# A new attention plan in a fused transformer block: V held still in four column tiles, row sums on VectorE, reciprocals through DRAM, and FFN chunks of 128 and 256 tokens

## The chip, the cores and the metric

The kernel runs on one core of one Trainium2 chip. The metric is the device time of a whole execution in microseconds (us); each figure is the median over the runs of a kernel. TensorE is called PE here, ScalarE ACT, VectorE DVE, GpSimd POOL, and SP is the engine that issues the DMA transfers. The *granted clock* is the share of full speed at which the chip let PE run.

## The reference, cut to what matters

One block with 2048 tokens of width 1024, all in bf16: layernorm, attention with 32 query heads of width 32 that share one key head and one value head, a residual, layernorm again, and a gated feed-forward network (FFN) of width 3584.

```python
q = (x @ wq) split into 32 heads          # x is the layernorm of A_x
k = x @ wk ; v = x @ wv                   # one head of width 32 for all
p = softmax(q @ k.T * 32 ** -0.5)         # 32 heads x 2048 x 2048
h = A_x + (p @ v) @ wo
g = layernorm(h) @ w_gate ; u = layernorm(h) @ w_up
out = h + (sigmoid(g) * u) @ w_down
```

The softmax takes 134 million exponentials. They are 1024 ACT instructions of 128 partitions x 1024 elements in both kernels.

## The kernel before

The Python that builds the kernel is a list scheduler: `pl.op(engine, instruction, deps, ...)` adds an operation with an assumed duration, and the scheduler fixes the order of instructions on every engine at build time. On the chip each engine runs its list in that order and waits on semaphores.

A *score visit* is one block of score matmuls followed by two exps. The exps write *slots* (tiles `Pr` in SBUF); a slot is free again when P V has read it. Scores have six PSUM banks. All other matmuls share two (`F_ps`), in *groups*: one group owns a bank until its result has been copied out. Score visits may come between any two matmuls of a group; another group may not.

Before, a slot holds 1024 elements per partition, and there are 16. Eight make a group of 4 heads x 128 queries. The probabilities are the stationary operand of P V, and the 33rd column of the moving V is ones, so the row sums come with the product and lie on the same partition as the queries that they divide:

```python
def mk_PV(G):
    def atoms(b):
        for j in range(4):                 # heads
            for kt in range(NT):           # 16 tiles of 128 keys
                mm(F_ps[:, b, j*VS : j*VS+DH+1], Pr[:, slot, co:co+P], Vaug[:, kt, 0:DH+1],
                   kt == 0, kt == NT - 1)
    def after(b, last):
        rL = DVE.reciprocal(ov[:, :, DH:DH+1])          # 4 elements a partition
        Osb = DVE.tensor_tensor(ov[:, :, 0:DH], rL broadcast, op=mult)
    first = lambda: [all exps of G] + [all of V]
    # (cut) a gate: V is complete, and earlier transposes are done; no reciprocal holds P V back
# (cut) then 4 PE transposes a half tile, a copy to OT, wo, layernorm,
# gate/up and down in 8 FFN chunks of 256 tokens
```

The loop that fills PE's list, the same in both kernels but for constants:

```python
while True:
    if can_s and run - t < 750.0: emit_S(v); v += 1; continue   # ACT nearly out of work
    if cur is not None: ...one more matmul of the running group...
    else: ...pick the first class in PRIO whose group is ready and whose gate is open...
    if can_s: emit_S(v) ...
# PRIO = xT, KV, Q0, PV, OTt, OP, hT, D, GU, Q;  can_s needs free slots
```

The softmax here doesn't subtract the row's maximum and nothing guards it: scores larger than these inputs give would overflow.

## Time and profile before

| | before |
|---|---|
| median of 2 runs | 1222.13 us (1219.03 to 1225.24) |
| span of the profiled run | 1223.8 us |
| PE / ACT / DVE busy | 96% / 85% / 26% |
| ACT's wait for scores | 25.9 us |
| start of the last exp | 1060.6 us |
| from the end of the last exp to the end | 162.2 us |

The page of the profiled run of the kernel before: its busy times, its busy tenths in 40 equal slices, and the exps' line (busy time, mean ns of one; then idle time before them and what ended it).

```profile
...
PE 1174.0 (96%) x22016; PEld 835.1 (68%) x22016; DVE 316.4 (26%) x838; ACT 1042.1 (85%) x1283; POOL 47.2 (4%) x109
...
PE   4899979999999999999999999999999999999999
...
DVE  8523321212222222223121222132222212232121
ACT  6899999999999999999999999999999989711120
...
PEclk9999989999999999999999999999999999999999
...
L495 ACT ACTIVATE Pr<-S_ps 128x1024 bf16<-128x1024 f32 x1024 | 972.4, 1052 | 26.4 <-PE S_ps L330 25.9
...
```

ACT is at eight or nine tenths until the 34th slice and, after the 35th, nearly idle, while PE goes on. The windows view of the same run, cut at the end of the last exp (busy us and instructions of each engine, then granted clock and DMA):

```profile
...
core 0: us, PE busy (x) PEld busy (x) DVE busy (x) ACT busy (x) POOL busy (x), PEclk, DMA share, GB/s
0.00:1061.60 1061.60, 1016.05 (x20773) 718.99 (x20774) 280.94 (x760) 1020.56 (x1227) 45.91 (x106) 0.99 0.41 117
1061.60:1223.80 162.20, 157.99 (x1245) 116.09 (x1243) 35.50 (x78) 21.54 (x57) 1.34 (x3) 1.00 0.63 164
...
```

ACT is busy for 1020.56 of the 1061.60 us of attention. The view of waits agrees (engine and line, then whom it waited for; us, times, longest):

```profile
...
engine line waited for: us in total, times, longest us
...
ACT Pr L495 <- PE S_ps L330: 25.9, 29, 2.2
...
```

PE's timeline after the last exp (start, duration, instructions):

```profile
...
1074.47 47.32 PE L330 MATMUL F_ps<-hnT,ring 128*128 128x256 bf16 x432
...
1123.48 24.34 PE L330 MATMUL F_ps<-zone,hact 128*128 128x512 bf16 x112
1147.65 49.07 PE L330 MATMUL F_ps<-hnT,ring 128*128 128x256 bf16 x448
1196.56 24.34 PE L330 MATMUL F_ps<-zone,hact 128*128 128x512 bf16 x112
```

These are gate/up and down of the last two chunks, dense. So attention is bounded by ACT, and the tail is PE work that did not fit beside it.

### The profile page before, as it was taken

What the parts mean: (1) busy time and instruction counts of PE and PEld (TensorE: products, weight loads), DVE (VectorE), ACT (ScalarE), POOL (GpSimd) and SP (SyncE); (2) the same over time, 40 slices, a digit from 0 to 9 for tenths busy, and PEclk for the clock granted to TensorE, in tenths of its full rate; (3) what the DMA queues carried; (4) which work ended last, traced back from release to release, by engine and by line L of the source; (5) the groups of instructions that cost most, each with busy time, mean ns of one, the idle gap of its engine ahead of it and who ended that gap; (6) DMA issues with size and microseconds to landing.
All of it is one profiled execution on the core that took longest, in us unless ns stands there. A gap on an engine that the chain in (4) does not pass through costs nothing.

```text
span 1223.8 us, 47137 instructions
## 1 busy us (share of the span) xinstructions
PE 1174.0 (96%) x22016; PEld 835.1 (68%) x22016; DVE 316.4 (26%) x838; ACT 1042.1 (85%) x1283; POOL 47.2 (4%) x109
## 2 busy tenths in 40 slices
PE   4899979999999999999999999999999999999999
PEld 3665557785678756877568675778657776587684
DVE  8523321212222222223121222132222212232121
ACT  6899999999999999999999999999999989711120
POOL 6100000000000000000000000000000000000000
PEclk9999989999999999999999999999999999999999
DMA  9411175562056601565016460256303653089390
GB/s 320 116 28 41 42 260 156 148 173 64 20 149 174 192 20 46 150 191 148 16 50 191 119 170 20 70 165 184 111 20 86 172 148 102 15 224 263 105 252 18
DMA packets 258612, 151.02 MB, mean 123 GB/s; under 512 B 7280, under 2 KB 248944, under 8 KB 258416
## 3 DMA queue, kind: packets, MB, share of 16 engines
q1 hardware_dynamic: 258416, 148.00, 43.1%
q8 instruction: 173, 2.83, 1.0%
q14 instruction: 23, 0.19, 0.0%
HBM read 140.64 MB, written 7.34 MB: 121 GB/s over the span
## 4 chain that ended last, share of the span: by engine, by line
PE 63%; ACT 31%; issue 3%; DVE 2%; POOL 0%; DMA 0%
PE F_ps L330 54%; ACT Pr L495 28%; PE S_ps L330 9%; ACT tnh L669 1%; ACT zone L313 1%; PE F_ps L619 0%; ACT zone L230 0%; DVE OT L566 0%; DVE st L274 0%; DVE st L276 0%; PE F_ps L558 0%; DMA ring<-in_A_x_dram 0%; POOL dsb L287 0%; DVE hnT L625 0%; DVE ring L307 0%
## 5 line engine op out<-in xcount | busy, mean ns | idle before, releaser
L495 ACT ACTIVATE Pr<-S_ps 128x1024 bf16<-128x1024 f32 x1024 | 972.4, 1052 | 26.4 <-PE S_ps L330 25.9
L330 PE MATMUL F_ps<-hnT,ring 128*128 128x256 bf16 x3584 | 440.6, 275 | 2.5 <-DVE OT L566 1.2
L330 PEld LDWEIGHTS F_ps<-hnT,ring 128*128 128x128 bf16 x3584 | 332.5, 98 | 61.3 <-issue 3.1
L330 PEld LDWEIGHTS F_ps<-Vaug,Pr 128*128 128x128 bf16 x8192 | 229.7, 96 | 28.1 <-issue 4.1
L330 PE MATMUL F_ps<-Vaug,Pr 128*128 128x33 bf16 x8192 | 244.4, 178 | 2.4 <-issue 1.5
L330 PE MATMUL S_ps<-QTb,kT 32*128 32x128 bf16 x8192 | 208.5, 218 | 15.4 <-ACT Pr L495 10.1
L330 PE MATMUL F_ps<-zone,hact 128*128 128x512 bf16 x896 | 213.2, 380 | 0.8 <-DVE OT L566 0.5
L330 PEld LDWEIGHTS S_ps<-QTb,kT 32*128 32x128 bf16 x8192 | 119.2, 93 | 127.9 <-ACT Pr L495 81.6
L676 DVE SCALAR_TENSOR_TENSOR hact<-tnh,F_ps 128x256 bf16<-128x256 f32 x224 | 94.3, 421 | 384.0 <-ACT tnh L669 383.9
L669 ACT ACTIVATE tnh<-F_ps 128x256 f32<-128x256 f32 x224 | 90.7, 405 | 115.0 <-PE F_ps L330 115.0
L330 PEld LDWEIGHTS F_ps<-zone,hact 128*128 128x128 bf16 x896 | 79.2, 98 | 91.3 <-DVE OT L566 0.7
L330 PE MATMUL F_ps<-zone 128*128 128x256 bf16 (+2 forms) x512 | 76.5, 292 | 3.1 <-POOL rstd L290 1.2
L707 DVE SCALAR_TENSOR_TENSOR h_sb<-F_ps,h_sb 128x512 bf16<-128x512 f32 x32 | 22.1, 692 | 203.1 <-PE F_ps L330 203.1
L330 PE MATMUL F_ps<-wo_sb,OT 128*128 128x512 bf16 x256 | 64.2, 381 | 3.8 <-DVE OT L566 3.7
L531 DVE RECIPROCAL rL<-F_ps 128x4 f32<-128x4 f32 x128 | 23.4, 183 | 133.7 <-PE F_ps L330 133.5
L330 PEld LDWEIGHTS F_ps<-zone 128*128 128x128 bf16 x512 | 37.5, 98 | 24.2 <-ACT zone L230 1.4
L284 POOL TENSOR_SCALAR zb<-mvb 128x1 bf16<-128x1 bf16 x32 | 7.5, 233 | 1026.4 <-DVE mvb L280 1026.1
L330 PEld LDWEIGHTS F_ps<-wo_sb,OT 128*128 128x128 bf16 x256 | 21.0, 97 | 28.4 <-DVE OT L566 6.9
L533 DVE TENSOR_TENSOR Osb<-F_ps,rL 128x128 bf16<-128x128 f32 x128 | 37.2, 291 | 3.8
L594 DVE TENSOR_TENSOR h_sb<-F_ps,xres 128x512 bf16<-128x512 f32 x32 | 22.1, 692 | 54.4 <-PE F_ps L330 54.4
L337 PE MATMUL F_ps<-ident,zone 128*128 128x128 bf16 x128 | 11.0, 236 | 17.3 <-POOL dsb L287 9.1
L231 DVE CAST hact<-F_ps 128x512 bf16<-128x512 f32 x24 | 16.6, 692 | 40.2 <-PE F_ps L330 40.2
(39 smaller groups left out, 232.4 us busy)
## 6 DMA issues: line engine op xcount, KB each, us to landing
ring<-in_B_w_gate_dram SPq DMA_DIRECT2D x112, 512.0 KB, 4.1
ring<-in_B_w_up_dram SPq DMA_DIRECT2D x112, 512.0 KB, 5.9
zone<-in_B_w_down_dram SPq DMA_DIRECT2D x4, 1792.0 KB, 15.4
ring<-in_A_x_dram SPq DMA_DIRECT2D x16, 256.0 KB, 7.0
xres<-in_A_x_dram SPq DMA_DIRECT2D x16, 256.0 KB, 2.7
out_dram<-h_sb SPq DMA_DIRECT2D x32, 128.0 KB, 1.7
q_scratch<-hact SPq DMA_DIRECT2D x24, 128.0 KB, 1.8
QTb<-q_scratch SPq DMA_DIRECT2D x6, 512.0 KB, 6.3
```

Of the source, the lines that this page charges most:

```text
L231: lambda: DVE.tensor_copy(out=out_ap, in_=in_ap))
L284: f = pl.op("pool", lambda: POOL.tensor_scalar(out=zb[:, ph, t:t + 1], in0=mvb[:, ph, t, 1:2], scalar1=LN_EPS_BF16, scalar2=None, op0=ALU. ...
L313: xnorm[t] = evac(lambda: ACT.activation(out=dst, in_=src, func=ACTF.Copy, scale=sc), lambda: DVE.tensor_scalar(out=dst, in0=src, scalar1= ...
L330: return lambda: PE.matmul(o, lhsT=l, rhs=r, start=start, stop=stop, **kw)
L337: return [(lambda dt=dt: PE.transpose(out=tp[:, dt * P:(dt + 1) * P], in_=xn[:, t % 2, dt * P:(dt + 1) * P], identity=ident[:, :]), P, []) ...
L495: exps[u] = pl.op("act", lambda slot=slot, pb=pb: ACT.activation(out=Pr[:, slot, :].rearrange("p (a b) -> p a b", a=2), in_=S_ps[:, pb:pb ...
L531: a = pl.op("dve", lambda: DVE.reciprocal(rL[:, k, :].unsqueeze(2), ov[:, :, DH:DH + 1]), [last], prio=0, occ=70, lat=280)
L533: e = pl.op("dve", lambda: DVE.tensor_tensor(out=Osb[:, hh % 2, (g % 4) * P:(g % 4 + 1) * P].rearrange("p (a b) -> p a b", a=4), in0=ov[:, ...
L594: h_ev[(t, dc)] = pl.op("dve", lambda: DVE.tensor_tensor(out=h_sb[:, t % 4, sl], in0=F_ps[:, b, :], in1=xres[:, t % 2, sl], op=ALU.add), [ ...
L669: a = pl.op("act", lambda: ACT.activation(out=tnh[:, k, :], in_=F_ps[:, b, 0:256], func=ACTF.Tanh, scale=0.5), [last, tn_user.get(k)], pri ...
L676: e = pl.op("dve", lambda: DVE.scalar_tensor_tensor(out=hactT[:, ft, :], in0=tnh[:, k, :], scalar=1.0, in1=F_ps[:, b, 256:512], op0=ALU.ad ...
L707: e = pl.op("dve", lambda: DVE.scalar_tensor_tensor(out=h_sb[:, t % 4, sl], in0=F_ps[:, b, :], scalar=0.5, in1=h_sb[:, t % 4, sl], op0=ALU ...
```

## The change

Its intent is to make P V cheaper on PE and to shorten the ends.

- V becomes the stationary operand, 32 columns wide, so four heads run side by side in four column tiles of the array and the moving operand is 256 probabilities. The product comes out transposed, as `wo` needs it, and the transposes of O go away.
- The ones column goes with it. DVE adds the probabilities of a group over the key tiles, a small group of matmuls (SUM) sums over partitions, and the reciprocals, which now lie on the wrong partitions, are broadcast through DRAM.
- A group is 8 slots of twice the size (4 heads x 256 score columns), and there are 12 slots (five more, in buffers that are not yet in use, serve at the start only). P V may be picked only when the reciprocals are nearly back by the builder's reckoning or, with at most one slot free, as soon as their load back has been issued there.
- The FFN's chunks are 128 tokens at both ends and 256 between, nine in place of eight.

The core of the diff, with cuts marked:

```diff
-    NPS = 16
+    NP = 12
-        Pr = SB("Pr", [NPS, 1024])
+        Pr = SB("Pr", [NP, 2048])
+        acc = SB("acc", [2, 2048])
 ...
+    add_op[(qi, kp, i)] = pl.op("dve", DVE.tensor_tensor(out=a, in0=in0, in1=slot[:, h], op=ALU.add), ...)
 ...
+    # SUM, then:
+    rc = pl.op("dve", DVE.reciprocal(r_sb[:, k, :], F_ps[:, b, 0:64]), ...)
+    r1 = dma(SP.dma_start(r_dram[k], r_sb[0:P:8, k, :]), ..., [rc], prio=0)
+    lds = [dma(SP.dma_start(rb[:, k, :], bass.AP(r_dram.tensor, r_dram.offset + k * 1024,
+               [[256, 4], [0, DH], [1, 256]])), ..., [r1, ot_ev.get(qi - 2)], prio=0)]
 ...
+    # P V, for kt, for j in 4 heads:
+    mm(F_ps[DH*j:DH*(j+1), b, 0:256], Vt[:, kt, :], s[:, j*512 + k2*256 : ...+256],
+       kt == 0, kt == NT - 1, tile_position=(0, DH * j))
+    def gate():
+        if qi not in rb_ld or any(o.end is None for o in rb_ld[qi]): return False
+        if len(free_slots) <= 1: return True
+        return rb_ld[qi][-1].end <= pl.free["pe"] + 1900.0
 ...
+    FC = [(0,)] + [(i, i + 1) for i in range(1, NT - 1, 2)] + [(NT - 1,)]
-    PRIO = ["xT", "KV", "Q0", "PV", "OTt", "OP", "hT", "D", "GU", "Q"]
+    PRIO = ["xT", "KV", "Q0", "SUM", "PV", "OP", "hT", "D", "GU", "Q1", "Q"]
-                if can_s and run - t < 750.0:
+                if can_s and run - t < 1000.0:
```

Left out here: the wider tanh (512 elements), layernorm statistics for several tiles at once, the order of the first loads, gate and up weights in quarters of a slab that are spaced out in time, three slabs for four, and the scheduler's assumed durations.

## The prediction

> **What bounds it now.** Two engines in turn. By the page, PE is busy 96% and ACT 85% of 1223.8 us. By the timelines the first score exp starts at 27.3 us and the last ends near 1061.6 us; in between ACT waits for scores only 25.9 us in all (view of waits). Eight exps take 7.57 us, so 1024 take 969 us. PE always has work too; what does not fit beside attention is left over: from 1061 to 1221 us it runs gate/up of two token chunks (47.3 and 49.1 us) and down projections (24.3 us each). So attention is ACT-bound, and the 162 us tail is PE backlog.
>
> **PE, costed by start-to-start rates of the timeline.** Score block of 16: 0.33 us. Old P V: 64 matmuls in 1.61 us, 25 ns each, 206 us in all. Gate/up: 448 in 49.07 us, 109 ns each.
>
> - Removed: old P V 206 us; the 128 transposes of O, 0.056 us each, 7 us.
> - Added: new P V, 16 rounds of four column tiles; I assume the four overlap fully, at 109 ns a round (estimate from the gate/up rate): 112 us, plus about 10 us of mode switches. Row-sum matmuls: 64 groups at about 0.35 us, plus the two raw groups: 26 us.
> - Unchanged: score, FFN and wo columns.
>
> Net PE saving 65 to 75 us.
>
> **ACT.** The exps stay 1024 of 1024 elements. Tanh becomes 98 of 512 and 28 of 256, about 60 us against 69. Attention still ends at about 1060.
>
> **DVE.** About 868 bf16 adds of 1024. The Trainium skill ("VectorE: DVE Perf Modes", the perf-mode tier table) gives bf16 tensor_tensor in SBUF two elements a cycle; here a bf16 PSUM copy of 1024 takes 691 ns, so I take 0.6 to 0.7 us each: 520 to 600 us. DVE goes from 316 us (26%) to about 800 us (70%), not binding.
>
> **DMA.** Nine FFN chunks instead of eight read 14.7 MB more. Each of 64 groups sends its reciprocal through DRAM and back, about 5 us, hidden while P V of that group is held back. The broadcast read has an outer size of 4; the skill ("DMA: Bandwidth & Descriptors", the rules table) says that confines it to four DMA engines; nothing here shows that yet.
>
> **Tail.** The last chunk has 128 tokens: its gate/up is 25 us of PE but 11 MB not yet loaded, at the 260 GB/s seen in the old tail 42 to 54 us. Last sums, round trip, P V, wo and layernorm: about 17 us; gate/up 46 to 50; down 12; output 3: about 80 us.
>
> **Sum.** 1060 + 80 + about 5 of backlog = 1145 us; 1105 to 1190 in 8 of 10.
>
> **What would show it.** Exps still 0.95 us each and ending at 1050 to 1070; new P V near 1.8 us a group; adds under 0.7 us; last gate/up phase waiting on DMA, PE visibly idle in it; mean PE share below 96%.
>
> **What would make it wrong.** The reciprocal's round trip late behind weight loads holds one of only two spare PSUM banks; PE is in order, so scores and exps starve. Column tiles overlapping less than fully (a round over 150 ns takes back 40 us). Adds at one element a cycle (1.1 us) would make DVE the bound.
>
> Faster by over 2%: 0.85; within 2%: 0.09; slower: 0.06.

## The result, and the profile after

The changed kernel takes 1297.41 us (median of 2 runs, 1297.25 to 1297.57). Its results are correct. Executions over 1.5% slower than the fastest of the same kernel are left out of the means. Ratios in this text are the mean time of one kernel's fast runs over that of the other's of the same rounds, so not quite the ratio of the medians. Here it is 1.0611, with a 95% interval of 1.0545 to 1.0678: slower by 6%. The prediction of 1145 us and its range of 1105 to 1190 us are both wrong, and so is the direction.

The page of the changed kernel, the same lines as before and the new ones:

```profile
...
PE 1145.6 (88%) x16632; PEld 694.3 (54%) x16704; DVE 840.1 (65%) x1450; ACT 1028.1 (79%) x1167; POOL 48.6 (4%) x89
...
PE   6879867879998999979997999889997999799967
...
DVE  8659855667767676676757776676757775764111
ACT  4759977879988997899979997899879997994010
...
PEclk9989978989999999989998999989998999899999
...
L567 ACT ACTIVATE Pr<-S_ps 128x1024 bf16<-128x1024 f32 x1014 | 965.3, 1037 | 119.8 <-PE S_ps L367 114.0
L544 DVE TENSOR_TENSOR acc<-acc,Pr 128x1024 bf16<-128x1024 bf16 x744 | 497.9, 688 | 126.8 <-ACT Pr L567 123.8
...
L367 PE MATMUL F_ps<-Pr,Vt 128*32 128x256 bf16 x4056 | 160.8, 299 | 0.5 <-DVE h_sb L859 0.5
...
```

Each exp is as long as it was (1037 against 1052 ns; ten more stand under the names of other buffers), and the adds take 688 ns as assumed. What differs is that ACT's row is full of eights and sevens, and that the granted clock dips again and again. The windows view of the changed kernel, cut at its own last exp:

```profile
...
core 0: us, PE busy (x) PEld busy (x) DVE busy (x) ACT busy (x) POOL busy (x), PEclk, DMA share, GB/s
0.00:1179.20 1179.20, 1048.75 (x15725) 627.99 (x15792) 820.15 (x1412) 1019.16 (x1147) 47.22 (x86) 0.95 0.45 131
1179.20:1295.50 116.30, 96.88 (x909) 66.34 (x912) 19.99 (x39) 8.97 (x21) 1.34 (x3) 0.96 0.59 171
...
```

ACT does the same work during attention, 1019.16 us against 1020.56, but attention takes 1179.2 us in place of 1061.6. The difference of 117.6 us is idle ACT (160.0 against 41.0 us, with 1.4 us less work). The tail is 45.9 us shorter. 117.6 less 45.9 is 71.7 us, the difference of the two spans. The view of waits says what ACT waited for:

```profile
...
engine line waited for: us in total, times, longest us
ACT Pr L567 <- PE S_ps L367: 114.0, 76, 14.0
...
```

114.0 against 25.9 us is 88 of the 118. The rest is mostly at the start and in waits for FFN results.

Now to a place where it happens. The timeline of the changed kernel, all engines, from a group's last exp on (the first of the four exps in the top line); S_ps is a score visit, `acc,sel` the SUM group, `zone,hact` a down projection, `Pr,Vt` P V:

```profile
...
644.96 3.99 ACT L567 ACTIVATE Pr<-S_ps 128x1024 bf16<-128x1024 f32 x4
...
648.67 0.42 PE L367 MATMUL F_ps<-acc,sel 128*32 128x64 bf16 x32
...
649.02 0.40 PE L367 MATMUL S_ps<-QTb,kT 32*128 32x256 bf16 x8
649.17 0.56 DVE L608 RECIPROCAL r_sb<-F_ps 128x64 f32<-128x64 f32 x1 [1.86 <-PE F_ps L367]
649.32 4.70 ACT L567 ACTIVATE Pr<-S_ps 128x1024 bf16<-128x1024 f32 x5
...
650.79 0.52 SPq L610 DMA_DIRECT2D r_scratch<-r_sb  x1
...
651.48 0.40 PE L367 MATMUL S_ps<-QTb,kT 32*128 32x256 bf16 x8
...
652.87 5.99 PE L367 MATMUL F_ps<-zone,hact 128*128 128x512 bf16 x27 [0.50 <-DVE hact L807]
...
654.46 0.54 SPq L611 DMA_DIRECT2D rb<-r_scratch  x1
...
658.79 0.40 PE L367 MATMUL F_ps<-Pr,Vt 128*32 128x256 bf16 x8
...
659.13 0.40 PE L367 MATMUL S_ps<-QTb,kT 32*128 32x256 bf16 x8
...
659.58 2.86 ACT L567 ACTIVATE Pr<-S_ps 128x1024 bf16<-128x1024 f32 x3 [5.56 <-PE S_ps L367]
...
```

The group's last exp ends at 646.0 us, its row sums are done at 649.1 and their reciprocals at 649.7. The store to DRAM is issued at 650.8, the load back at 654.5. Where the builder picked PE's next group, P V's gate was still shut, so it picked a down projection of 28 matmuls, which starts at 652.87 us (one record is missing in the trace). Up to 658.79 us there is no score visit among them, although a visit may come between any two of its matmuls and ACT runs dry at 654.0 us. P V starts at 658.79, a visit follows after its first two rounds, and ACT has stood idle for 5.56 us. That is exactly what one expects if no slot was free until P V had released one.

It can be counted. A visit loads 8 blocks of score weights and a P V group 64 blocks of V, and the trace has the record of every load. At the start of 60 of the 64 P V groups exactly 12 visits had begun whose slots no P V had read: all slots were taken. ACT's idle time before the first exp after each of these 60 starts adds up to 78 us of the 114.0. From a group's last exp to the start of its P V it takes 8.2 us in the median, while the four spare slots keep ACT busy for 7.6 us (eight exps). Before the change it took 1.6 us in the median, and the spare slots were worth the same eight exps.

The builder itself says so. By the builder's own assumed durations the kernel before ends at 1207 us and the changed one at 1273 us, 62 of the 64 P V groups are picked with no slot free, and ACT is out of work with no slot free for 73 us. The builder knows neither the granted clock nor late transfers. By its durations the order alone gives 66 of the 72 us between the two spans, and for every kernel of the table below its plan ends only 0.2 to 3.0% before the measured time. The experiments test the slots on the chip.

### The profile page after: what moved, and what is told of

Its sections match the earlier page's. It is cut to its first block, busy times and chain, and to the rows that moved or that the text cites. A ratio compares the mean times of both kernels' runs of the same rounds, so it can differ in the third digit from the quotient of the medians.

```text
span 1295.5 us, 38388 instructions
## 1 busy us (share of the span) xinstructions
PE 1145.6 (88%) x16632; PEld 694.3 (54%) x16704; DVE 840.1 (65%) x1450; ACT 1028.1 (79%) x1167; POOL 48.6 (4%) x89
## 4 chain that ended last, share of the span: by engine, by line
PE 68%; ACT 11%; DVE 8%; DMA 7%; issue 6%; SPq 1%; DVEq 0%
PE F_ps L367 58%; ACT Pr L567 10%; PE S_ps L367 10%; DMA ring<-in_B_w_up_dram 3%; DVE acc L544 2%; DVE hact L807 2%; DMA rb<-r_scratch 2%; DMA r_scratch<-r_sb 1%; SPq L758 1%; DMA ring<-in_B_w_gate_dram 1%; DVE st L312 1%; DVE h_sb L859 1%; DVE st L314 0%; DMA out_dram<-h_sb 0%; DVE zone L253 0%
## 5 line engine op out<-in xcount | busy, mean ns | idle before, releaser
L567 ACT ACTIVATE Pr<-S_ps 128x1024 bf16<-128x1024 f32 x1014 | 965.3, 1037 | 119.8 <-PE S_ps L367 114.0
L544 DVE TENSOR_TENSOR acc<-acc,Pr 128x1024 bf16<-128x1024 bf16 x744 | 497.9, 688 | 126.8 <-ACT Pr L567 123.8
L367 PE MATMUL F_ps<-hnT,ring 128*128 128x256 bf16 (+1 forms) x4032 | 452.7, 264 | 42.9 <-DMA ring<-in_B_w_up_dram 13.7
L367 PE MATMUL S_ps<-QTb,kT 32*128 32x256 bf16 x4096 | 210.7, 281 | 51.1 <-ACT Pr L567 50.1
L367 PE MATMUL F_ps<-Pr,Vt 128*32 128x256 bf16 x4056 | 160.8, 299 | 0.5 <-DVE h_sb L859 0.5
L367 PEld LDWEIGHTS F_ps<-Pr,Vt 128*32 128x32 bf16 x4056 | 101.1, 104 | 52.1 <-issue 42.0
L807 DVE SCALAR_TENSOR_TENSOR hact<-tnh,F_ps 128x512 bf16<-128x512 f32 x98 | 67.1, 684 | 58.8 <-PE F_ps L367 57.3
L544 DVE TENSOR_TENSOR acc<-Pr 128x1024 bf16<-128x1024 bf16 x122 | 78.3, 664 | 10.0 <-ACT Pr L567 8.8
L367 PE MATMUL F_ps<-zone 128*128 128x512 bf16 (+3 forms) x563 | 75.4, 282 | 3.9 <-ACT QTb L252 1.3
L832 ACT ACTIVATE tnh<-F_ps 128x256 f32<-128x256 f32 x28 | 10.9, 390 | 78.6 <-PE F_ps L367 78.6
L834 DVE SCALAR_TENSOR_TENSOR hact<-tnh,F_ps 128x256 bf16<-128x256 f32 x28 | 11.6, 416 | 49.6 <-ACT tnh L832 49.6
```

The costliest lines, as they stand in the source:

```text
L367: return lambda: PE.matmul(o, lhsT=l, rhs=r, start=start, stop=stop, **kw)
L544: add_op[(qi, kp, i)] = pl.op("dve", lambda: DVE.tensor_tensor(out=a, in0=in0, in1=slot[:, h], op=ALU.add), [exp_of[(qi, kp, i)]] + dp, pr ...
L567: exps[u] = pl.op("act", lambda i=i, pb=pb: ACT.activation(out=slot[:, i * 1024:(i + 1) * 1024].rearrange("p (a b) -> p a b", a=2), in_=S_ ...
L807: e = pl.op("dve", lambda: DVE.scalar_tensor_tensor(out=hact[:, sg * 512:(sg + 1) * 512], in0=tnh[:, k, :], scalar=1.0, in1=F_ps[:, b, :], ...
L832: a = pl.op("act", lambda: ACT.activation(out=tnh[:, k, 0:256], in_=F_ps[:, b, 0:256], func=ACTF.Tanh, scale=0.5), [last, tn_user.get(k)] ...
L834: e = pl.op("dve", lambda: DVE.scalar_tensor_tensor(out=hact[:, sg * 256:(sg + 1) * 256], in0=tnh[:, k, 0:256], scalar=1.0, in1=F_ps[:, b, ...
```

## The experiments

Four explanations were on the table. **A**: the slots. A group keeps its 8 of 12 slots until P V, P V waits for the trip through DRAM and then behind whatever FFN group is running, and meanwhile the builder has no slot for a score visit. **B**: the trip is later on the chip than the builder reckoned, and the in-order PE stands still at a held bank. **C**: DVE, 65% busy, delays what PE needs. **D**: the 128-token chunks wait for weights. The first four kernels ran on one chip, the next four on another, the last three on a third, each beside the kernel before.

| run | median us | ratio to before (95%) | ACT's wait for scores, us | last exp starts, us |
|---|---|---|---|---|
| before | 1222.13 | 1 | 25.9 | 1060.6 |
| changed | 1297.41 | 1.0611 (1.0545 to 1.0678) | 114.0 | 1178.2 |
| e1_no_wait | 1292.71 | 1.0546 (1.0497 to 1.0594) | 108.5 | 1171.6 |
| e2_no_trip | 1215.81 | 0.9931 (0.9893 to 0.9969) | 29.7 | 1081.4 |
| e3_short_adds | 1297.97 | 1.0597 (1.0548 to 1.0647) | 112.4 | 1173.0 |
| e4_ten_slots | 1456.81 | 1.1902 (1.1851 to 1.1952) | 176.1 | 1351.4 |
| e5_not_held | 1300.98 | 1.0651 (1.0611 to 1.0691) | 56.8 | 1105.8 |
| e6_break_in | 1252.74 | 1.0252 (1.0217 to 1.0288) | 61.2 | 1116.7 |
| e7_pairs | 1275.17 | 1.0436 (1.0400 to 1.0472) | 110.3 | 1166.4 |
| e8_ones | 1221.48 | 0.9995 (0.9959 to 1.0031) | 17.6 | 1073.1 |
| e9_ones_pairs | 1179.99 | 0.9643 (0.9615 to 0.9672) | 23.8 | 1073.0 |
| e10_break_pairs | 1234.98 | 1.0102 (1.0067 to 1.0137) | 74.3 | 1123.9 |
| e11_no_pacing | 1173.95 | 0.9586 (0.9553 to 0.9618) | 25.3 | 1075.4 |

### Is the chip late, or is the order itself at fault?

```diff
-   in1=rb[:, qi % 2, :]...
+   in1=rstd[:, 0, 0:1] broadcast          # a constant; results wrong on purpose
+   # after the order is fixed: this multiply no longer waits for the load of rb
```

> The changed kernel with the very same instruction order, but the multiply that finishes P V reads a constant and no longer waits for the reciprocals that come back from DRAM (results wrong on purpose; the transfers still run). Theory A (the order itself starves ScalarE: score visits are not in the instruction stream where they are needed, because all slots for probabilities are taken): 1280 to 1298 us, ratio to the changed kernel at least 0.985, ScalarE still idle for about 100 us before score exps. Rival B (the round trip is later on the chip than the plan reckoned, so the spare PSUM bank is held and the in-order PE stands still): 1150 to 1220 us.

1292.71 us; ACT still waits 108.5 us for scores. The order was the same and the trip's lateness could no longer stop PE, so B is not the cause: the intervals of this run and of the changed kernel overlap, so the 4.7 us between the medians are not clear of noise.

### Does the trip through DRAM make the bad order?

```diff
-   r1 = dma(... r_dram <- r_sb ...); lds = [dma(... rb <- r_dram ...)]
-   rb_ld[qi] = lds
+   rb_ld[qi] = [rc]                       # the reciprocals are used where they lie
-   in1=rb...
+   in1=r_sb broadcast                     # wrong partitions: results wrong on purpose
```

> The reciprocals are used in SBUF where they are computed, with no trip through DRAM (results wrong on purpose, since they stand on the wrong partitions); the plan orders the instructions anew, so P V is no longer held back for the trip. Theory A: slots come free sooner, the last exp ends at 1065 to 1090 us in place of 1179, the wait of ScalarE for scores falls from 114 us to under 45, and the whole takes 1190 to 1225 us. Rival C (VectorE's adds or the four-column P V itself slow attention): still over 1260 us.

1215.81 us, 82 less than the changed kernel. The wait for scores fell to 29.7 us and the last exp starts 97 us earlier:

```profile
...
ACT Pr L567 <- PE S_ps L367: 29.7, 26, 10.5
...
```

All 12 slots are taken at the start of 8 P V groups, no longer of 60. The adds and the four-column P V are all still there, so C falls for the greater part here.

### Are DVE's adds in the way?

```diff
-   DVE.tensor_tensor(out=a, in0=in0, in1=slot[:, h], op=ALU.add)
+   DVE.tensor_tensor(out=a[:, 0:128], in0=in0[:, 0:128], in1=slot[:, h][:, 0:128], op=ALU.add)
```

> The changed kernel with the very same order, but each row-sum add on VectorE covers 128 elements in place of 1024 (results wrong on purpose), so VectorE loses some 450 us of work. Theory A: within 1.5% of the changed kernel, 1278 to 1300 us. Rival C (VectorE at 65% with adds in front of evacuations is what holds PE up): 1150 to 1230 us.

1297.97 us, no change. The larger group of adds took 162.7 us in place of 497.9, and the time did not notice. DVE is not what holds the changed kernel in this order.

### Is it the number of slots?

```diff
-    NP = 12
+    NP = 10
```

> The changed kernel with 10 slots for probabilities in place of 12, nothing else, ordered anew. Theory A: a group fills 8 slots, so only 2 are left for the next group while the first waits for its reciprocals; ScalarE's idle time before score exps rises by 100 us or more and the time is 1390 to 1480 us. Rivals B and C: slots are not the limit, 1290 to 1320 us.

1456.81 us, 159 more, for two slots. The wait of ACT for scores rose by 62 us only, less than the 100 expected; the last exp is 173 us later, and ACT's waits for the 512-wide gate products, counted apart, rose from 30.0 to 105.1 us. The time is inside the range that A gave and far from the other's. More than 12 slots cannot be tried in this layout: with 13 the kernel does not build, for want of room in SBUF.

### What if P V is not held back?

```diff
-   if qi not in rb_ld or any(o.end is None for o in rb_ld[qi]): return False
-   if len(free_slots) <= 1: return True
-   return rb_ld[qi][-1].end <= pl.free["pe"] + 1900.0
+   return qi in rb_ld
```

> The trip through DRAM is kept, but the rule that holds P V back until its reciprocals are due is dropped: P V may start as soon as its sums are done, and its result then waits in its PSUM bank for the reciprocals. Theory A1 (the holding rule costs the time): 1200 to 1235 us, ScalarE's wait for scores under 60 us. Theory A2 (the trip costs it in any place: the wait moves from the slots to one of two spare PSUM banks): 1260 to 1300 us, hardly any change, with PE waiting more on the multiply after P V.

1300.98 us, no gain, as A2 said, but not quite in A2's way: attention did get shorter (the wait for scores is 56.8 us, the last exp 72 us earlier), and the tail got as much longer. The timeline of this run, one P V and what follows on PE, with DVE's multiply that empties P V's bank:

```profile
...
610.30 1.93 PE L367 MATMUL F_ps<-Pr,Vt 128*32 128x256 bf16 x64
...
612.17 0.28 PE L367 MATMUL F_ps<-hnT,ring 128*128 128x256 bf16 x1
...
616.30 1.58 PE L367 MATMUL F_ps<-hnT,ring 128*128 128x256 bf16 x13
...
618.70 0.42 DVE L640 TENSOR_TENSOR OT<-F_ps,rb 128x256 bf16<-128x256 f32 x1 [1.32 <-DMA rb<-r_scratch]
...
619.27 0.93 PE L367 MATMUL F_ps<-hnT,ring 128*128 128x256 bf16 x7 [0.63 <-DVE OT L640]
...
```

P V starts at 610.30 us and its bank is emptied at 619.12, because the multiply waits for the DMA. For 8.8 us the FFN has one bank in place of two. Over the whole run:

```profile
...
PE F_ps L367 <- DVE OT L640: 23.4, 29, 2.6
...
```

In the changed kernel it was 8.5 us:

```profile
...
PE F_ps L367 <- DVE OT L640: 8.5, 6, 2.9
...
```

So the FFN falls behind, and what it does not finish beside attention is done after it. That one bank is the reason for all of the lost FFN time is argued from these lines, not shown by a run of its own.

### What if P V may break into an FFN group?

```diff
+   if cur is not None and cur[0].cls not in ("SUM", "PV") and cur_i and not held:
+       banks = [the other bank, if it is free]
+       for cl in ("SUM", "PV") if banks else ():
+           if (first group of cl is ready and its gate open): set cur aside, run that group first
```

> The holding rule and the trip are kept, but row sums and P V may break into a running FFN group (a down projection is 28 matmuls, about 6 us) when the other spare bank is free. Theory A3 (half of the starvation is P V that is ready and stands behind an unbreakable FFN group): ScalarE's wait for scores falls from 114 us to 40 to 70 us, the time to 1215 to 1250 us. If the trip alone is to blame: over 1275 us.

1252.74 us, 45 less; the wait for scores, 61.2 us, is in the range expected, the time just above the 1215 to 1250 us. The holding rule and the trip were kept, so standing behind the FFN group is a real part of it, and not all: 55 of the 64 P V groups still start with all 12 slots taken.

### What do the 128-token chunks cost?

```diff
-    FC = [(0,)] + [(i, i + 1) for i in range(1, NT - 1, 2)] + [(NT - 1,)]
+    FC = [(i, i + 1) for i in range(0, NT, 2)]
```

> The FFN takes 8 chunks of 256 tokens again, as before the change; the attention plan stays as changed. If the 128-token chunks at both ends cost time (each loads all gate and up weights, 14.7 MB, for half the work, and PE waits in order for them): 1255 to 1280 us, 20 to 40 us less, with PE's waits on those weights falling from 27 us to under 10 us. If they help the tail as the change intends: 1300 us or more.

1275.17 us, 22 less. PE's wait for the up weights fell from 13.7 to 2.6 us. The wait for scores hardly changed, so this is a second cause beside the slots.

### A correct version without the trip

```diff
-   c_sel: sel[:, i, 8*i:8*i+8] = 1.0        # block i of the sums to rows 8i..8i+7
+   c_sel: sel = 1.0 everywhere              # each of the 32 rows of a head gets the sum
-   SUM group, reciprocal of 64, store to DRAM, load from DRAM
+   # at the end of P V's own group, into the other half of its bank:
+   mm(F_ps[DH*j:DH*(j+1), b, 256:512], sel[:, 0, :], acc[...256 columns...], ...)
+   rc = DVE.reciprocal(rb[:, qi % 2, :], F_ps[:, b, 256:512])
+   # P V's gate: the adds of its group exist
```

> A correct way without the trip: the row sums are taken with a stationary block of ones, so each of the 32 partitions of a head gets the sum, in the second half of P V's own PSUM bank; VectorE takes 256 reciprocals for 64 (about 1.7 us a group for 0.55) and no sum crosses DRAM. Theory A: last exp at 1062 to 1085 us, ScalarE's wait for scores under 45 us, 1210 to 1240 us in all, results right. If the longer reciprocals take back the gain through VectorE or the bank: over 1260 us.

1221.48 us with correct results: 76 less than the changed kernel, the same as before the change. ACT is fed again:

```profile
...
ACT Pr L565 <- PE S_ps L365: 17.6, 36, 2.4
...
```

The last exp starts at 1073.1 us. But 147 us follow it, and the timeline of PE shows what they are (gate/up of tiles 13 and 14, their down projection, then the last tile):

```profile
...
1074.57 1.93 PE L365 MATMUL F_ps<-Pr,Vt 128*32 128x256 bf16 x64
1076.33 0.39 PE L365 MATMUL F_ps<-acc,sel 128*32 128x256 bf16 x8
...
1082.51 22.97 PE L365 MATMUL F_ps<-hnT,ring 128*128 128x256 bf16 x208
...
1132.14 24.35 PE L365 MATMUL F_ps<-zone,hact 128*128 128x512 bf16 x112 [0.34 <-DVE hact L817]
1156.33 6.71 PE L365 MATMUL F_ps<-hnT,ring 128*128 128x128 bf16 x112
...
1205.82 12.25 PE L365 MATMUL F_ps<-zone,hact 128*128 128x512 bf16 x56
```

Gate/up of the pair lasts to 1131, nearly all of it after attention; its down projection lasts 24 us; and the last tile's gate/up takes from 1156.33 to 1205.82, 49.5 us for 448 matmuls of 128 columns, waiting on weights; and its down projection 12 us.

### Both remedies, and without the spacing of the weights

e9 is e8 with the eight pairs of e7. e11 is e9 with one more edit:

```diff
-   f"sl{sl}{w}{hf}", D * SW, deps, prio=4, pace=True))
+   f"sl{sl}{w}{hf}", D * SW, deps, prio=4))
```

> Both remedies together, results right: row sums by a block of ones with no trip through DRAM, and eight FFN chunks of 256 tokens. If starvation for slots and the weights of the two small chunks are the two separate causes, their gains add: from 1297 by about 76 (ones) and 22 (pairs) us to 1180 to 1205 us, under both kernels, last exp near 1075 us, and the tail after it 105 to 115 us, bounded by PE in gate/up and down of the last pair. If they overlap: 1210 us or more.

> As the kernel with ones and pairs, but the gate and up weights are asked for as soon as their slab is free, without the spacing tied to ScalarE's progress. If the spacing keeps the tail's weights late: 5 to 12 us less than with it. If it protects other transfers: no gain, or a loss.

e9 takes 1179.99 us: the two gains add, and more than add (117 us; 76 and 22 are 98). e11 takes 1173.95 us, a further 6 us; the intervals of the two ratios just touch, but each of the six runs of e11 (at most 1175.27 us) is below each of the five of e9 (at least 1177.66), and the cause is visible. The end of e11's PE timeline:

```profile
...
1096.94 49.07 PE L365 MATMUL F_ps<-hnT,ring 128*128 128x256 bf16 x448 [1.02 <-DVE hnT L747]
1146.07 24.12 PE L365 MATMUL F_ps<-zone,hact 128*128 128x512 bf16 x109
```

The last gate/up runs without a gap, 49.07 us. In e9 the same 448 matmuls took from 1094.57 to 1151.05 us, with waits on the weights. e11 is faster than both kernels, by 4% than before the change, with correct results.

### Breaking in together with pairs

The edits of e6 and e7 together; the trip and the holding rule stay.

> The trip and the holding rule kept, row sums and P V allowed to break into FFN groups, and pairs. If the trip still costs something once nothing else stands in front of P V: 20 to 40 us more than the kernel with ones and pairs, 1205 to 1240 us. If breaking in removes all of it: the same within 10 us.

1234.98 us, 55 more than e9, more than the 20 to 40 expected though inside the range in us. So the trip, with the holding rule that belongs to it, still costs where P V may break into an FFN group. It may do so only when the other bank is free, so this run does not show a P V that never waits for the FFN: 60 of the 64 still start with all 12 slots taken.

## Why the prediction was wrong

- **"Each of 64 groups sends its reciprocal through DRAM and back, about 5 us, hidden while P V of that group is held back."** This is the step that failed. Holding P V back hides nothing: P V is what frees the slots. Eight of 12 are filled by one group, so four visits, each two exps of 0.95 us, are 7.6 us of cover from a group's last exp. P V began 8.2 us after it in the median, and 12.8 us after it in the timeline shown; ACT's wait for scores rose from 25.9 to 114.0 us. The 5 us were too few as well: from the end of the reciprocal to the last semaphore update of the load back, the trace has 7.5 us in the median (4.9 to 11.3). That the read back is confined to four DMA engines ("DMA: Bandwidth & Descriptors", the rules table) fits the trace: each of the 64 loads raised its semaphore 5 times, once about 1 us after the issue and four times at the landing, and each store 16 times. Taking the trip away gave 82 us (e2), 76 with correct results (e8); taking away the holding alone moved the wait to a PSUM bank (e5).
- **What it did not ask at all**: how long the slots last. 16 slots for a group of 8 became 12 for a group of 8, but a slot now holds two exps, so the cover is the same 7.6 us as before; what grew is the time that it must cover, from 1.6 to 8.2 us in the median. Two slots fewer cost 159 us (e4). I counted busy time and durations, and no buffer's lifetime, and I did not ask the builder, whose own plan is 66 us longer.
- **"The reciprocal's round trip late behind weight loads holds one of only two spare PSUM banks; PE is in order, so scores and exps starve."** The starving was named, its cause was not: without the wait for the late transfers the time fell by 4.7 us, within noise (e1). The order fixed at build time already had the holes, 73 us of them for want of a slot in the builder's own plan.
- **"1060", the end of attention**: 1179.2 us. With the trip gone, 1074 (e8), so that attention is bounded by ACT was nearly right once the slots come free in time; no run says where the 12 us over the kernel before come from.
- **"About 80 us" of tail and "about 5 of backlog"**: 116.3 us in the changed kernel. The last gate/up, predicted at 46 to 50, took 50 (1230.1 to 1280.5 us). The term that was mis-sized is the backlog. The chunk of tiles 13 and 14 cannot begin before tile 14 leaves attention, and PE worked on its gate/up (with the last P V and wo between) until 1206 us, 27 us after the last exp, and then 24 us on its down projection. In e8, with attention shorter, nearly all of this gate/up lies after attention, and 147 us follow the last exp.
- **"Net PE saving 65 to 75 us"**: PE's busy time fell by 28 us, from 1174.0 to 1145.6. Part of the gap can be the clock of the last point below; no run separates it.
- **Right: P V.** "1.8 us a group": in e8 the 64 matmuls take 1.76 us from start to the next group (1074.57 to 1076.33), 110 ns for each round of four, so the four column tiles overlap fully. The Trainium skill ("TensorEngine Tiling (Array Packing)", Theoretical Speedup) gives up to 4x for a dimension of at most 32; this trace agrees.
- **Right: the adds.** 688 ns each. "VectorE: DVE Perf Modes" (the perf-mode tier table) has bf16 tensor_tensor at two elements a cycle, and the trace agrees. DVE at 65% was not a bound (e3).
- **A follow-on that I left out: the clock.** The mean granted clock fell from 0.993 to 0.954. "TensorE: Matmul & The Clock Gate" (Part 1) says that PE falls to half rate after an idle window of about 3.4 us. The trace agrees on the half rate (near 182 us, 48 matmuls of P V took 2.75 us in place of 1.49) but not on the idle window: the clock fell 22 times within the changed kernel's work, and in the 3.4 us before each fall PE was busy for 0.8 to 1.8 us and never idle for more than 2.3 us at a stretch. Half clock lasted 119 us in all (17 us before the change), with PE busy for 95 of them. An estimate from this: full clock would save at most half of the 95. What the clock costs by itself no run isolates; with ACT fed (e9) it is 0.987.

What stays open is how the trip's cost divides between the holding rule, the bank and the FFN group: e5, e6 and e10 show that each is only another place for the same wait, not how large each would be alone. What the lower clock adds stays open too.

## What to carry to other kernels

When a change puts a new latency between a producer and the consumer that frees its buffers, count the buffers in time units: those left after one full set, times the producer's pace, must exceed that latency plus the longest piece of work that can stand in front of the consumer. An average busy share says nothing about it. Where a program fixes its order at build time, read the idle time out of its plan before predicting. A wait that is moved off one resource lands on the next one that is held (slots here, then PSUM banks), so shorten the wait itself: a sum that is computed in the layout where it is used needs no trip.

## What the Trainium skill lacked or had wrong

- "VectorE: DVE Perf Modes" explains reciprocal by iterative-divide steps with a repeat count of 8 and gives no time for it. Here 64 fp32 elements from PSUM took 551 ns and 256 took 1755, so 6.3 ns for each further element. An estimate with the page's clock of 0.96 GHz: 6.0 cycles, fewer than eight.
- "DMA: Bandwidth & Descriptors" gives the fixed cost of one transfer, about 2.0 us, as measured on the gpsimd path. Here a 4 KB store from SP, beside weight loads, landed in 1.7 to 4.7 us, 2.8 in the median; the load back of 128 KB landed 3.8 us after its issue in the median, and the whole trip took 7.5 us. A dependent pair through DRAM has to be planned with such numbers.
- "TensorEngine Tiling (Array Packing)" says that a change of tiling mode drains the array, without a time. In the changed kernel's trace weight loading stands idle for 0.21 us, with no releaser that the profile names, at 668 of 1166 changes. Whether this is the drain no run shows.
- "TensorE: Matmul & The Clock Gate" gives no figure for how little work in a window costs the full clock. Here falls came after windows of 3.4 us with 0.8 to 1.8 us of busy PE.
- No page treats the choice between a partition broadcast through DRAM and a matmul with a block of ones. Here the second was better by 76 us (e8), although its reciprocals are four times as many.
